# Linear attention followed by a two-layer network, one core: the store of x is queued right behind its multiplication, and the pools of on-chip memory begin at other addresses

## The chip, the cores and the metric

The kernel runs on one core of one Trainium2 chip. The metric is the device time of one execution in microseconds (us). The time before is the median of three runs, 1118.28 us (1115.12 to 1119.28).

## What is computed

Eight batches of eight heads, 576 positions, 64 values a head; then a network on the 4608 rows of 512 values that the attention gives.

```python
def phi(x):
    proj = np.einsum('bhsd,df->bhsf', x, w_phi)          # 64 -> 128 features
    proj = proj - np.max(np.abs(proj), axis=-1, keepdims=True)
    return np.concatenate([np.exp(proj), np.exp(-proj)], axis=-1)
q_p, k_p = phi(q), phi(k)
kv  = np.einsum('bhsf,bhsd->bhfd', k_p, v)
z   = np.sum(k_p, axis=2)
num = np.einsum('bhsf,bhfd->bhsd', q_p, kv)
den = np.einsum('bhsf,bhf->bhs', q_p, z)[..., None] + 1e-06
attn = num / den
# x: attn with the heads side by side, 4608 x 512
h = x @ w_in            # 512 -> 2048
g = h - np.tanh(h)
out = g @ w_out         # 2048 -> 512
```

## The kernel before

There are two stages. The first does the attention, unit by unit: a unit is two heads of one batch, and there are 32. The second does the network for nine groups of 512 rows, each in 16 steps over 128 of the 2048 hidden values.

**The first stage is a software pipeline written out by hand** (`manual_schedule`: each engine takes its instructions in the order of the code). `ramp` starts units 0 to 2, `period(i)` is called for i = 3 to 31, `drain` ends it. One call of `period` works on six units at once: `a` is unit i (projected), `c` is i-1, `p` is i-2 (its numerator is made), `r` is i-3 (its denominator is made and loaded), `q` is i-4 (its reciprocals are spread), `o` is i-5 (multiplied and stored).

The way of one unit through the steps that matter here:

- `num` (L327, PE) multiplies q's features with kv into the PSUM tile `po`. `num_copy` (L351, ACT) copies `po` into the tile `d`. `d` has three buffers (`bufs=3`), so the copy for unit p can only write once the buffer of unit p-3, which is `o`, has been stored.
- The bank of `po` is also the bank of `pa`: the last part of the next unit's `project` (L219, PE, `pa`) writes there, and so waits for `num_copy`.
- `denom` (L341, PE) and `ksum` (L299, PE) write the bank `pu`. `denom_copy` (L355, ACT) copies the denominators to `dd`, one buffer, out of the pool `tail`.
- `den_recip_load` (L360, a DMA on SP's queue) brings one row in 32 of `dd` into `dn`, nine numbers a partition; `den_recip` (L365, DVE) makes `rn`; `den_store` (L370, SP) writes it to `rr` in DRAM; a period later `den_spread` (L375, two DMAs on SP) reads `rr` back into `rb`, spread over 64 partitions a head.
- A period later again `den_mul` (L378, POOL) multiplies `d` by `rb` in place, and `x_store` (L381, SP) writes `d` to `xs` in DRAM, from where the second stage loads it. `rb` has one buffer, so the spread of unit q comes behind the multiplication of unit o.

SP's queue takes its DMAs in the order of the code: an instruction that waits holds those behind it. SP also loads `v` (L200). The loads of q and k (`qk`, L196) and of the weights (`rawi`, `rawo`) are issued by ACT.

**The second stage** keeps x and the weights as pairs of a high and a low part, three matmuls of 512 columns for each product (L606 for the first layer, L649, L650 and L652 for the second), with the polynomial and tanh on ACT and DVE and the split of g on ACT and POOL.

**Memory.** Pools are laid one behind the other along a partition: `consts`, `tail`, `wpool`, `wpa`, `xp0`, and behind them the pools of the first stage (`raw`, `p1`, `p2`), whose room the second stage's pools (`xp`, `wp`, `gp`, `gm`) take over. Tiles of `wpool`, `wpa`, `xp0`, `raw` and of the second stage are 2048 bytes a partition or multiples of it. In the kernel before `wpool` begins 1056 bytes past a multiple of 2048, and so do all these tiles. In `p1` the tiles `zt` (512 bytes) and `ones` (128 bytes) lie ahead of the two `kp` (10240 bytes each), which so begin 1696 bytes past one.

Of the kernel before, what the change touches and what calls it, by code (L numbers as in the profile page):

```python
# [8 lines left out]
F32 = mybir.dt.float32  # L9
# [10 lines left out]
P = 128  # L20
# [12 lines left out]
def tile_linear_attention_moe(  # L33
# [26 lines left out]
    CH = S // 2  # L60
# [3 lines left out]
    consts = ctx.enter_context(tc.tile_pool(name="consts", bufs=1))  # L64
# [1 line left out]

    ident = consts.tile([P, P], F32, name="ident")
    make_identity(nc, ident)
    bias_t = consts.tile([P, 4], F32, name="bias_t")
    nc.gpsimd.memset(bias_t[:, 0:1], PB1)  # L70
    nc.gpsimd.memset(bias_t[:, 1:2], PB2)
    nc.gpsimd.memset(bias_t[:, 2:3], -Y0)
# [1 line left out]
    tail = ctx.enter_context(tc.tile_pool(name="tail", bufs=2))  # L74
# [8 lines left out]
    def split_w(n, pin=lambda ins: ins):  # L83
        d, nm, f = (wi, wo)[n % 2], "io"[n % 2], n // 2
        early = f < AHEAD
        w = d[f]
        wh = (wpa if early else wp[0]).tile([P, DM], F32R, name=f"wh{nm}{f}")
        wl = wpool.tile([P, DM], F32R, tag="w", name=f"wl{nm}{f}")
        if early or nm == "i":
            pin(nc.scalar.copy(wh, w))  # L90
        else:
            pin(nc.vector.tensor_copy(wh, w))
        d[f] = (wh, wl)

        def low():
            pin(nc.gpsimd.tensor_tensor(wl, w, f32(wh), ALU.subtract))

        return low
# [25 lines left out]
    with ExitStack() as c1:  # L124
        raw = c1.enter_context(tc.tile_pool(name="raw", bufs=2))
        p1 = c1.enter_context(tc.tile_pool(name="p1", bufs=1))
# [65 lines left out]
        def load(u, queue=nc.sync):  # L192
            u.qk = p2.tile([P, PC], F32, tag="qk", name=f"qk{u.i}")
            cut = (0, PC) if u.i else (0, 4 * P, PC)
            for o, w in zip(cut, cut[1:]):
                queue.dma_start(u.qk[:, o:w], qkT[u.i][:, o:w])  # L196
# [6 lines left out]
        def project(u, parts):  # L203
            for part in parts:
                if part == "j":
                    u.t = [p2.tile([P, 2, 5, F], F32, tag="t0", name=f"t{u.i}_0"), None]
                    u.m = [p2.tile([P, 2, 5], F32, tag="m0", name=f"m{u.i}_0"), p2.tile([P, 2, 4], F32, tag="m1", name=f"m{u.i}_1")]
                    u.pj = ps_pj.tile([P, 2, 512], F32, tag="pj", name=f"pj{u.i}")
                    bank, tiles = u.pj, range(4)
                elif part == "t":  # L210
                    u.pt = ps_t.tile([P, 2, 512], F32, tag="pt", name=f"pt{u.i}")
                    bank, tiles = u.pt, range(4, 5)
                else:
                    u.pa = ps_d.tile([P, 2, 512], F32, tag="po", name=f"pa{u.i}")
                    bank, tiles = u.pa, range(5, 9)
                for k, a in enumerate(tiles):
                    for e in range(2):
                        hs = slice(e * D, (e + 1) * D)
                        nc.tensor.matmul(  # L219
                            bank[:, e, k * F : (k + 1) * F], u.qk[hs, a * P : (a + 1) * P], wph[hs, :], start=True, stop=True  # L220
                        )
# [10 lines left out]
        def centre(u, parts):  # L232
            for part in parts:
                x, m, t = part_of(u, part)
                nc.vector.tensor_reduce(m, x, AX.X, ALU.max, apply_absolute_value=True)  # L235
                nc.vector.tensor_tensor(t, x, m.unsqueeze(3).broadcast_to(list(t.shape)), ALU.subtract)  # L236
# [49 lines left out]
        def kadd(u):  # L286
            x = p2.tile([P, 2, 2, F], F32, tag="ss", name=f"ss{u.i}")
            nc.gpsimd.tensor_tensor(x, u.kp[:, :, 1], u.kp[:, :, 2], ALU.add)
            nc.gpsimd.tensor_tensor(x, x, u.kp[:, :, 3], ALU.add)
            nc.gpsimd.tensor_tensor(x, x, u.kp[:, :, 4], ALU.add)  # L290
            nc.gpsimd.tensor_tensor(x, x, u.kp[:, :, 0], ALU.add)
            u.ss = x
# [14 lines left out]
        def ksum_turn(u):  # L307
            nc.tensor.transpose(u.pu[:, 0:F], u.kst, ident)
# [42 lines left out]
            nc.scalar.copy(u.d.rearrange("p (c n) -> p c n", c=2), u.po[:, :, 0:CH])  # L351

        def denom_copy(u):
            u.dd = tail.tile([P, CH], F32, tag="dd", name=f"dd{u.i}", bufs=1)
            nc.scalar.activation(u.dd, u.pd, AF.Identity, bias=bias_t[:, 3:4])  # L355

        def den_recip_load(u):
# [19 lines left out]
        def den_mul(u, pin=lambda ins: ins):  # L377
            pin(nc.gpsimd.tensor_tensor(u.d, u.d, u.rb, ALU.mult))  # L378

        def x_store(u):  # L380
            nc.sync.dma_start(xs[u.b // 2][u.hp, :, (u.b % 2) * S : (u.b % 2 + 1) * S], u.d)  # L381

        units = []
        for i in range(B * NHP):
            u = Unit()
# [13 lines left out]
        def unit(i):  # L399
            return units[i] if 0 <= i < NU else None  # L400

        def bank():
            return ps_c.tile([P, 512], F32, tag="pu", name="pu")
# [48 lines left out]
        def period(i):  # L452
            a, c, p, r, q, o = (unit(i - n) for n in range(6))
            w = dec[i - 3]
            low = split_w(i - 4) if 4 <= i < 2 * AHEAD + 4 else None
            if o:
                den_mul(o)
            project(a, "jat" if i > 3 else "ajt")
            centre(a, "jt")
            kadd(c)  # L460
            if low:
                low()
            dec.append(dec_load(i - 2, nc.scalar))
            if i + 2 < NU:
                load(units[i + 2], nc.scalar)
            pu = bank()
            if r:
                denom(r, pu)
            ksum(p, pu)
            if r:  # L470
                denom_copy(r)
                den_recip_load(r)
            if q:
                den_spread(q)
            if o:
                x_store(o)
            if i > 3:
                load_v(a)
            ksum_copy(p)
            kv_turn(p)  # L480
            kv_turn_copy(p)
            dec_0(w, a.pt)
            q_turn(c)
            ksum_turn(p)
            q_turn_rest(c, pu)
            q_exp(c)
            q_exp_rest(c)
            ksum_turn_copy(p)
            centre(a, "a")
            k_exp(a, 0)  # L490
            kv(c)
            kv_copy(c)
            k_exp(a, 1, (0,))
            dec_1(w)
            dec_2(w)
            if r:
                den_recip(r)
                den_store(r)
            dec_3(w)
            if i == NU - 1:  # L500
                for j in range(NCT // 2):
                    x_split(xt[0], j)
            if i == NU - 2:
                xt[0] = x_tiles(0)
                for j in range(NCT):
                    x_load(0, xt[0], j)
            num(p)
            num_copy(p)
            if i < NU - 1:
                k_exp(a, 1, (1,))  # L510
# [9 lines left out]
        def drain():  # L520
            o, q, r, p, c = units[-5:]
            den_mul(o)
            pu = bank()
            denom(r, pu)
            ksum(p, pu)
            denom_copy(r)
            den_recip_load(r)
            den_spread(q)
            x_store(o)
            ksum_copy(p)  # L530
            k_exp(c, 1, (1,))
            kadd(c)
            den_mul(q)
            dec.append(dec_load(NU - 2, nc.scalar))
            kv_turn(p)
            kv_turn_copy(p)
            decode(dec[NU - 3], lambda: (den_recip(r), den_store(r)))
            q_turn(c)
            ksum_turn(p)
            q_turn_rest(c, pu)  # L540
            q_exp(c)
            ksum_turn_copy(p)
            q_exp_rest(c)
            kv(c)
            kv_copy(c)
            num(p)
            x_store(q)
            den_spread(r)
            den_mul(r)
            dec.append(dec_load(NU - 1, nc.scalar))  # L550
            for j in range(NCT // 2, NCT):
                x_split(xt[0], j)
            kv_turn(c)
            kv_turn_copy(c)
            pu = bank()
            ksum(c, pu)
            denom(p, pu)
            ksum_copy(c)
            num_copy(p)
            decode(dec[NU - 2])  # L560
            ksum_turn(c)
            ksum_turn_copy(c)
            denom_copy(p)
            den_recip_load(p)
            x_store(r)
            num(c)
            w = dec[NU - 1]
            dec_0(w, ps_t.tile([P, 2, 512], F32, tag="pt", name="pt"))
            num_copy(c)
            dec_1(w)  # L570
            dec_2(w)
            dec_3(w)
            denom(c, bank())
            denom_copy(c)
# [11 lines left out]
    with ExitStack() as c2:  # L586
# [86 lines left out]
        for i in range(len(steps) + 2):  # L673
            if i < len(steps):
                g, f = steps[i]
# [13 lines left out]
            if 1 <= i <= len(steps):  # L689
                g, f = steps[i - 1]  # L690
# [12 lines left out]
            if i >= 2:  # L703
                g, f = steps[i - 2]
# [61 lines left out]
```

## Time and profile before

| what | before |
|---|---|
| median of three runs | 1118.28 us (1115.12 to 1119.28) |
| profiled execution | 1114.96 us, of which its span is 1113.2 us and 1.8 us lie around it |
| granted TensorE clock | 0.998 |
| first stage | from 0 to 321.4 us of the span |
| second stage | from 321.4 us to the end |
| PE busy | 1096.1 us, 98% of the span |
| DVE busy | 837.9 us |
| ACT busy | 770.6 us |
| POOL busy | 441.0 us |

The span runs from the first to the last instruction of the profiled execution. PE is the matmul engine, PEld its weight load, DVE the vector engine, ACT the scalar engine, POOL the third compute engine and SP the engine that here issues DMAs only; SPq and ACTq are the instruction queues ahead of those engines. An entry such as "ACT d L351 <- DMA xs<-d" reads: ACT's instruction of line 351, which writes d, waited for the DMA that writes xs from d.

### The profile page before, as it was taken

The numbers are of one execution on the slowest core, as the hardware profiler recorded it, in microseconds if no ns is written. First come the engines' busy times: TensorE is split into PE (matmuls) and PEld (weight loads), VectorE is DVE, ScalarE is ACT, GpSimd is POOL, SyncE is SP. The second block draws the span as 40 slices with busy tenths as digits, with TensorE's granted clock in tenths as the row PEclk, the third lists the DMA queues.
The fourth block names the chain that finished last, engine by engine and source line by source line (L and its number), as shares of the span: only waits on it lengthen the run. The fifth ranks groups of instructions, "written<-read, shape, count | busy, mean of one in ns | idle before, by whom it ended". The sixth has DMA issues, their size and how long they took to land.

```text
span 1113.2 us, 18532 instructions
## 1 busy us (share of the span) xinstructions
PE 1096.1 (98%) x6956; PEld 864.5 (78%) x6956; DVE 837.9 (75%) x1166; ACT 770.6 (69%) x1394; POOL 441.0 (40%) x349
## 2 busy tenths in 40 slices
PE   8999999999999999999999999999999999999998
PEld 6676666676668888888888888888888888888886
DVE  6988889899988767767667767767767676676664
ACT  5787887777777766667666666666666666666664
POOL 4787877666645532322222222222222222222222
PEclk9999999999999999999999999999999999999999
DMA  5577777677740011011011010001002002000001
GB/s 184 168 207 208 214 209 216 207 220 221 204 144 1 1 54 34 22 49 39 1 38 38 1 38 38 1 10 66 1 1 76 1 1 76 1 1 38 1 1 39
DMA packets 51003, 85.46 MB, mean 77 GB/s; under 512 B 13280, under 2 KB 24672, under 8 KB 50912
## 3 DMA queue, kind: packets, MB, share of 16 engines
q1 hardware_dynamic: 36656, 52.02, 14.6%
q10 hardware_dynamic: 14256, 32.25, 9.9%
q8 instruction: 55, 0.90, 0.3%
q14 instruction: 36, 0.29, 0.1%
HBM read 65.08 MB, written 19.02 MB: 76 GB/s over the span
## 4 chain that ended last, share of the span: by engine, by line
PE 91%; DMA 2%; DVE 2%; ACT 2%; SPq 1%; POOL 1%; issue 1%; ACTq 0%; DVEq 0%; POOLq 0%
PE ph L606 34%; PE po L649 12%; PE po L652 12%; PE po L650 12%; PE pc L278 5%; PE po L327 4%; PE pu L341 3%; PE pa L219 3%; PE pj L219 3%; DMA xs<-d 2%; PE ptt L247 2%; PE pc L316 1%; DVE t L236 1%; DVE m L235 1%; PE pu L299 1%; ACT d L351 1%
## 5 line engine op out<-in xcount | busy, mean ns | idle before, releaser
L635 POOL TENSOR_TENSOR gl<-s,gh 128x512 fp32r<-128x512 f32 x144 | 186.1, 1293 | 556.0 <-ACT gh L634 547.5
L613 ACT ACTIVATE y<-ph 128x512 f32<-128x512 f32 x144 | 86.2, 598 | 254.2 <-PE ph L606 254.2
L622 DVE SCALAR_TENSOR_TENSOR s<-s,y 128x512 f32<-128x512 f32 x144 | 102.1, 709 | 186.5 <-ACT s L615 185.5
L649 PE MATMUL po<-who,gh 128*128 128x512 f32 x572 | 223.3, 390 | 1.8 <-ACT gh L634 1.8
L606 PE MATMUL ph<-xh,whi 128*128 128x512 f32 x576 | 224.3, 389 | 0.0
L606 PE MATMUL ph<-xh,wli 128*128 128x512 f32 x576 | 224.1, 389 | 0.0
L606 PE MATMUL ph<-xl,whi 128*128 128x512 f32 x576 | 224.1, 389 | 0.0
L650 PE MATMUL po<-wlo,gh 128*128 128x512 f32 x572 | 223.0, 390 | 0.0
L652 PE MATMUL po<-who,gl 128*128 128x512 f32 x572 | 153.7, 391 | 0.0
L628 DVE COPY_PREDICATED s<-mk,th 128x512 f32<-128x512 uint32 x128 | 122.8, 959 | 13.8 <-DVE th L627 0.9
L649 PEld LDWEIGHTS po<-who,gh 128*128 128x128 f32 x572 | 107.7, 188 | 25.1 <-ACT gh L634 2.7
L606 PEld LDWEIGHTS ph<-xh,whi 128*128 128x128 f32 x576 | 108.0, 188 | 23.3 <-DVE s L628 0.5
L606 PEld LDWEIGHTS ph<-xl,whi 128*128 128x128 f32 x576 | 108.2, 188 | 22.4
L652 PEld LDWEIGHTS po<-who,gl 128*128 128x128 f32 x572 | 108.0, 189 | 22.6
L606 PEld LDWEIGHTS ph<-xh,wli 128*128 128x128 f32 x576 | 108.1, 188 | 22.4
L650 PEld LDWEIGHTS po<-wlo,gh 128*128 128x128 f32 x572 | 107.6, 188 | 22.3
L615 ACT ACTIVATE s<-y,bias_t 128x512 f32<-128x512 f32 x144 | 104.4, 725 | 0.5 <-POOL gl L635 0.5
L621 ACT ACTIVATE mk<-y,bias_t 128x512 f32<-128x512 f32 x144 | 103.5, 719 | 1.4 <-DVE s L628 1.4
L625 DVE SCALAR_TENSOR_TENSOR s<-s,ph 128x512 f32<-128x512 f32 x144 | 98.9, 686 | 5.2
L624 DVE SCALAR_TENSOR_TENSOR s<-s,s 128x512 f32<-128x512 f32 x128 | 88.8, 694 | 15.9 <-ACT s L617 3.5
L272 ACT ACTIVATE kp<-t 128x1024 f32<-128x1024 f32 (+1 forms) x128 | 90.5, 731 | 8.9 <-DVE t L236 7.8
L617 ACT ACTIVATE s<-y,bias_t 128x512 f32<-128x512 f32 x128 | 92.4, 722 | 0.9 <-POOL gl L635 0.9
(98 smaller groups left out, 1693.7 us busy)
## 6 DMA issues: line engine op xcount, KB each, us to landing
qk<-in_qkT ACTq DMA_DIRECT2D x27, 576.0 KB
v<-in_v SPq DMA_DIRECT2D x32, 320.0 KB, 4.2
rb<-rr SPq DMA_DIRECT2D x64, 144.0 KB, 3.6
xs<-d SPq DMA_DIRECT2D x32, 288.0 KB, 3.5
out<-o SPq DMA_DIRECT2D x36, 256.0 KB, 2.3
rawo<-in_moe_w_out ACTq DMA_DIRECT2D x16, 512.0 KB, 3.9
rawi<-in_moe_w_in ACTq DMA_DIRECT2D x15, 512.0 KB, 4.1
xl<-xs SPq DMA_DIRECT2D x24, 256.0 KB, 3.2
```

The lines of the kernel that those rows point to most:

```text
L272: nc.scalar.activation(u.kp[h, :, j, s, :], u.t[r][h, :, x, :], AF.Exp, scale=1.0 - 2.0 * s)
L606: nc.tensor.matmul(h, wt[:, c * P : (c + 1) * P], x[:, c, 0:N], start=(i == 0), stop=(i == 3 * NCT - 1))
L615: nc.scalar.activation(s1, y, AF.Square, bias=bias_t[:, 0:1])
L617: nc.scalar.activation(s2, y, AF.Square, bias=bias_t[:, 1:2])
L621: nc.scalar.activation(mk, y, AF.Relu, bias=bias_t[:, 2:3])
L622: nc.vector.scalar_tensor_tensor(s1, s1, PC1, y, ALU.add, ALU.mult)
L625: nc.vector.scalar_tensor_tensor(gs, gs, PA, h, ALU.mult, ALU.mult)
L628: nc.vector.copy_predicated(gs, mk.bitcast(U32), hh)
L635: pin(nc.gpsimd.tensor_tensor(gl, gs, f32(gh), ALU.subtract))
L649: nc.tensor.matmul(po[t], a, wo[f][0], start=(f == 0), stop=False)
L650: nc.tensor.matmul(po[t], a, wo[f][1], start=False, stop=False)
L652: nc.tensor.matmul(po[t], gl[:, t * P : (t + 1) * P], wo[f][0], start=False, stop=(f == NF - 1))
```

## The change

Three edits.

1. `x_store(o)` is called right behind `den_mul(o)`, at the head of `period` and of `drain`. Before it stood behind `den_recip_load(r)` and `den_spread(q)`. Those two now stand behind it in SP's queue.
2. The tile `dd` (1152 bytes a partition) comes from `p1`, a pool of the first stage alone, and no longer from `tail`. It has one buffer as before.
3. `bias_t` is 28 columns wide and no longer 4 (96 bytes more a partition). The columns that are written and read are the same four. Together with edit 2 this takes 1152 - 96 = 1056 bytes out from ahead of `wpool`: it, `wpa`, `xp0`, `raw` and the second stage's tiles begin at multiples of 2048 bytes. The first `kp` begins 640 bytes past one.

```diff
-    bias_t = consts.tile([P, 4], F32, name="bias_t")
+    bias_t = consts.tile([P, 28], F32, name="bias_t")
...
         def denom_copy(u):
-            u.dd = tail.tile([P, CH], F32, tag="dd", name=f"dd{u.i}", bufs=1)
+            u.dd = p1.tile([P, CH], F32, tag="dd", name=f"dd{u.i}")
...
         def period(i):
             if o:
                 den_mul(o)
+                x_store(o)
...
                 den_recip_load(r)
             if q:
                 den_spread(q)
-            if o:
-                x_store(o)
             if i > 3:
                 load_v(a)
...
         def drain():
             den_mul(o)
+            x_store(o)
             pu = bank()
...
             den_recip_load(r)
             den_spread(q)
-            x_store(o)
```

SP's queue in one call of `period` (i = 7), the kernel before and after as one piece of the difference; `xs<-d` is the store of unit o, `dn<-dd` the load of unit r's denominators, `rb<-rr` the two DMAs that spread unit q's reciprocals, `v<-in_v` the load of unit a's v, and `rr<-rn` the store of unit r's reciprocals. The numbers behind the names are buffers.

```order
 L370 DMA rr_851<-rn_849 128x9
-L360 DMA dn_924<-dd_922 128x1x9
-L375 DMA rb_926<-rr_851 64x576 x2
 L381 DMA xs_76<-d_602 128x576
+L360 DMA dn_925<-dd_923 128x1x9
+L375 DMA rb_927<-rr_851 64x576 x2
 L200 DMA v_930<-in_v 128x640
```

The store has moved ahead of three DMAs, and they now stand behind its wait for POOL.

The same queue at the head of `drain`, where o is unit 27; the last row is the store of unit 28.

```order
-L360 DMA dn_4107<-dd_4105 128x1x9
-L375 DMA rb_4109<-rr_4072 64x576 x2
 L381 DMA xs_79<-d_3829 128x576
+L360 DMA dn_4108<-dd_4106 128x1x9
+L375 DMA rb_4110<-rr_4072 64x576 x2
 L370 DMA rr_4135<-rn_4133 128x9
 L381 DMA xs_79<-d_3960 128x576
```

Here too the store has passed the load and the two spreads. The order of instructions on PE, ACT, DVE and POOL is the same in both kernels.

## The prediction

> **What bounds the kernel now.** I read the head of the page first, for the span and the busy time of each engine, then the chain of work that ended last.
>
> ```profile
> span 1113.2 us, 18532 instructions
> PE 1096.1 (98%) x6956; PEld 864.5 (78%) x6956; DVE 837.9 (75%) x1166; ACT 770.6 (69%) x1394; POOL 441.0 (40%) x349
> PE 91%; DMA 2%; DVE 2%; ACT 2%; SPq 1%; POOL 1%; issue 1%; ACTq 0%; DVEq 0%; POOLq 0%
> ```
>
> PE carries 91% of the chain, so only time in which PE waits, or a faster PE, can move the end. The chain also passes through DMA, SP's queue and ACT (2 + 1 + 2%): somewhere a transfer holds PE up. The busy time by stage tells where. I cut the span at the end of two copies of L355, one in each turn of `period`, and at the first matmul of L606.
>
> ```profile
> core 0: us, PE busy (x) PEld busy (x) DVE busy (x) ACT busy (x) POOL busy (x), PEclk, DMA share, GB/s
> 0.00:40.47 40.47, 34.60 (x381) 24.85 (x382) 28.61 (x36) 24.23 (x45) 19.70 (x27) 1.00 0.51 161
> 40.47:301.45 260.98, 257.56 (x2946) 179.67 (x2945) 234.24 (x326) 205.52 (x393) 194.82 (x150) 1.00 0.71 210
> 301.45:321.40 19.95, 17.76 (x179) 10.49 (x176) 17.09 (x24) 14.77 (x32) 11.34 (x9) 1.00 0.64 211
> 321.40:1095.00 773.60, 773.50 (x3414) 639.82 (x3411) 551.91 (x775) 518.92 (x916) 211.28 (x162) 1.00 0.07 24
> ```
>
> In the second stage PE is busy for 773.50 of 773.60 us: nothing that only removes waits can help there. In the steady part of the first stage PE is also nearly full, but busy time takes in the modelled tails of matmuls, so I look at the waits of just that stretch (40 to 302 us).
>
> ```profile
> POOL d L378 <- DMA rb<-rr: 24.6, 18, 1.9
> PEld pa L219 <- ACT d L351: 5.0, 10, 1.0
> ACT d L351 <- DMA xs<-d: 4.0, 10, 0.7
> PE pa L219 <- ACT d L351: 2.7, 4, 0.8
> ACT d L351 <- PE pj L219: 2.4, 2, 1.3
> ```
>
> Here is the stall: PE's `pa`, and the weight load ahead of it, wait for `num_copy` (L351), and `num_copy` waits for a store of x that has not landed. One such turn in order of time, on SP, POOL and ACT, and then the chain through it:
>
> ```profile
> 199.86 1.42 POOL L378 TENSOR_TENSOR d<-d,rb 128x576 f32<-128x576 f32 x1 [1.79 <-DMA rb<-rr]
> 204.07 0.51 ACT L355 ACTIVATE dd<-pu,bias_t 128x288 f32<-128x288 f32 x1 [1.88 <-PE pu L299]
> 204.60 0.59 SPq L360 DMA_DIRECT2D dn<-dd  x1
> 205.37 1.19 SPq L375 DMA_DIRECT2D rb<-rr  x2
> 206.60 1.30 SPq L381 DMA_DIRECT2D xs<-d  x1
> 210.07 0.32 SPq L370 DMA_DIRECT2D rr<-rn  x1
> 211.24 0.64 ACT L351 COPY d<-po 128x576 f32<-128x576 f32 x1 [1.31 <-PE pj L219]
> ```
> ```profile
> 210.04 1.11 PE pj L219 x16
> ...
> 211.24 0.65 ACT d L351
> ...
> 211.93 1.16 PE pa L219 x16
> ```
> ```profile
> DMA to landing us min/median/max: 4.5/4.5/4.5
> ```
>
> The product was ready at 199.86 + 1.42 = 201.28. Its store was issued at 206.60: SP stood at the load of `dd`, which waited for ACT until 204.58, and then issued the spread. The store took 4.5 us to land (last row: that store alone), to 211.1, and `num_copy` began at 211.24. The wait's label, PE's `pj`, is the last semaphore event, but the landing fits the start to 0.1 us, so I count this row of 2.4 us with the 4.0.
>
> **The change part by part. The store moved (edit 1).** It can now be issued at about 201.3, 5.3 us earlier. Landing took 3.1 to 5.6 us in this stretch:
>
> ```profile
> L381 SPq DMA_DIRECT2D xs<-d x26: 583/585/1565, 51.9 to 293.8; - x26
> ...
> DMA to landing us min/median/max: 3.1/3.5/5.6
> ```
>
> Even with the longest it lands at 206.9, well before the copy of this turn can start. The copy needs the numerator, whose matmuls end with the start of `pj` at 210.04, so some 3 us are left. The wait goes. What is late next? Turns in which the store happened to be in time show it, four in a row, and one that waited:
>
> ```profile
> 157.34:166.69 9.35, 9.35 (x111) 6.58 (x109) 8.34 (x13) 7.90 (x16) 7.82 (x7) 1.00 0.78 228
> 166.69:176.11 9.42, 9.42 (x111) 6.56 (x110) 8.61 (x13) 7.28 (x15) 7.82 (x7) 1.00 0.73 215
> 176.11:185.53 9.42, 9.42 (x111) 6.55 (x110) 8.61 (x13) 7.28 (x16) 6.58 (x6) 1.00 0.71 215
> 185.53:194.96 9.43, 9.43 (x111) 6.58 (x110) 8.63 (x13) 7.30 (x16) 6.55 (x6) 1.00 0.69 215
> 204.58:215.21 10.63, 9.84 (x112) 6.64 (x110) 8.85 (x14) 7.39 (x15) 6.57 (x6) 1.00 0.69 199
> ```
>
> In the first four PE has no gap, DVE has 0.8 to 1.0 us to spare, and ACT and POOL more. So PE is next, at 9.35 us for the shortest turn and 37.62 / 4 = 9.405 for the four. The steady stretch holds 27 turns (one `num_copy` each):
>
> ```profile
> L351 ACT COPY d<-po x27: 620/638/640, 45.9 to 297.5; 128x576 f32<-128x576 f32 x27
> ```
>
> Its mean turn is 260.98 / 27 = 9.666 us. At 9.405 the gain is 27 x 0.261 = 7.0 us, at 9.35 it is 27 x 0.316 = 8.5 us. PE's own waits for the copy, 5.0 + 2.7 = 7.7 us, lie between. I take 7.5. The lower bound is 4.0 us, what the list of waits puts down to the store by name, if PE's other waits for the copy only change their cause.
>
> **What the store is moved past.** The load of `dd` and the two spreads now stand behind the store's wait for POOL. POOL ended at 201.28 and the load could not go before 204.58: 3.3 us of room, of which issuing the store takes SP 0.58 us in the median and 1.57 at most. At least 1.7 us are left, so load and spread go out when they did. The spread needed that product in any case, as `rb` has one buffer. On the DMA engines the store's 288 KB now come ahead of the load and the spread, not behind them. With a median landing of 3.5 us it has landed by 204.8, when the spread's first DMA is 0.6 us from issue: cost between 0 and the 1.5 us by which the longest landing (206.9 against 205.37) would run into it. I take 0, since POOL, which waits for the spread, has 1.5 us or more idle in each quoted turn. The load of `v` follows the spread directly, about 1.2 us sooner; no row has anybody waiting for it. I take 0.
>
> At the head of `drain` the room is smaller:
>
> ```profile
> 306.81 1.42 POOL L378 TENSOR_TENSOR d<-d,rb 128x576 f32<-128x576 f32 x1 [2.25 <-PE po L327]
> 308.28 0.50 ACT L355 ACTIVATE dd<-pu,bias_t 128x288 f32<-128x288 f32 x1
> 310.89 0.59 SPq L381 DMA_DIRECT2D xs<-d  x1
> ```
>
> The product ends at 308.23, the denominators' copy at 308.78. With 0.59 us for the issue the load goes out 0.05 us late, with 1.57 us 1.0 us late, once. PE does not read what it brings before the second stage, so I count 0 and keep 1.0 us for the range.
>
> **`dd` in another pool, `bias_t` wider (edits 2 and 3).** No instruction is added, and the copy to `dd` reads and writes as many bytes (0.51 us). What they change is addresses. The stage where that could matter is the second. There 3414 matmuls fill 773.60 us, 226.6 ns each, 0.443 ns a column of 512. In the first stage the numerator's matmuls did better per column:
>
> ```profile
> 160.65 1.94 PE po L327 x16
> ```
>
> 1.94 us / 16 / 288 columns is 0.421 ns. If the second stage's extra 0.022 ns a column came from where its tiles begin, 512 columns would take 215.6 ns, and 3414 x 11.0 ns = 37.6 us would go. What speaks against it: the numerator's `qe` lies at no multiple of 2048 either, and the slices of `kp` that L278 streams are 1024 bytes each, starting 1696 bytes past a multiple of 2048, so every second one crosses such a boundary.
>
> ```profile
> L278 PE MATMUL pc<-kp,v x286: 378/379/431, 159.8 to 294.8; 128*64 128x256 f32 x143
> ```
>
> From the least to the median is 1 ns: crossing costs nothing there. But those are other matmuls, and no tile of the second stage lies elsewhere, so the trace can't exclude it. I take 0 and keep 37.6 us as a rival; a loss of the same kind has no row at all.
>
> The Trainium skill (TensorE: Matmul & The Clock Gate, Back-to-back issue gap) has N/2.4 + 2.5 ns between warm matmuls, about 216 ns for 512 columns, and names no address in it; the measured 226.6 ns is above that, so by the Trainium skill there is something in this stage to win, an estimate of 3414 x 10.8 = 36.9 us. The Trainium skill (SBUF — State Buffer, Terms) has lines of 16 bytes in this memory; 1056 is a multiple of 16, so by the Trainium skill every tile began on a line already and the layout changes nothing. No run here shows either.
>
> **The sum.** 7.5 us out of the first stage, 0 for the rest. The profiled execution would go from 1114.96 to 1107.5 us. It lies 3.3 us below the median of the runs, just under the lowest of them. As the stall hangs on when a transfer lands, some of those 3.3 us may be the same stall; I count 0.8 of it, an estimate. 1118.28 - 7.5 - 0.8 gives 1110.0 us, 0.7% faster. About 0.5% (5.6 us) is what a measurement of this kernel tells from no change.
>
> **The rivals.** *Another wait takes the place.* If in turn after turn without the stall DVE or ACT fall behind, only the 4.0 us booked by name go: 1114.3 us, no change that can be told. For it speaks that DVE fills 8.3 to 8.6 of 9.4 us; against it the four turns in a row without a gap on PE. *The addresses speed up the second stage.* 37.6 us more: 1110.0 - 37.6 = 1072.4 us. For it speaks the rate per column, against it L278's row and `qe`. *SP is held by POOL: slower.* If products end later than the denominators' copy less the issue, the load goes out late. It is issued at 204.60, and the store of the reciprocals made of it at 210.07, 5.5 us later, so it has 1.4 us of slack if it lands in 4 us, more than the store's median for 288 KB. It decides when POOL's product comes 1.7 + 1.4 = 3.1 us later than now; DVE then stands in front of its reciprocal, and each us beyond costs up to 27 us. With one us a turn: 27 - 7.5 = 19.5 us more, 1137.8 us. POOL waited 1.9 us for the spread at worst, and that is inside the 3.3 us already, so it is unlikely. *The change does nothing*, the store being issued no earlier, would need a product that ends after 206: no quoted turn has it.
>
> **How the numbers follow.** Forecast (1106 to 1113 us) 0.69; another wait in its place 0.17; addresses speed up the second stage 0.09; SP held by POOL, or addresses that cost, 0.05. A few of the first case's hundredths (0.04) fall short of 0.5%. Faster: 0.69 + 0.09 - 0.04 = 0.74. Same: 0.17 + 0.04 = 0.21. Slower: 0.05. The range leaves out the two rivals far away (0.14) and a little at either end: low 1105, which is 1118.28 less 8.5 and less the 3.3 us between profile and median, with 1.5 us for scatter; high 1117, which takes in the case of another wait.
>
> **What would show it.** In the profile after, SP issues the store before the load of `dd`, about 0.1 us behind POOL's product. "ACT d <- DMA xs<-d" and "pa <- ACT d" are gone from the list of waits. The turns take 9.35 to 9.45 us throughout, the first matmul of L606 comes at about 314 us, and the second stage takes 773.6 us as before. I am wrong if the turns still exceed 9.5 us with another releaser, if matmuls of the second stage are spaced by other than 226.6 ns, or if the load of `dd` is issued more than 1 us behind its copy.

## The result, and the profile after

Six runs of the changed kernel take 1110.24 us in the median (1109.98 to 1110.71), six of the kernel before 1116.29 us (1114.06 to 1119.28). The ratio is 0.9941, 95% interval 0.993 to 0.9953: 0.6% faster. The runs after lie within 0.7 us, those before within 5.2 us. The profiled execution takes 1110.15 us, where that of before took 1114.96.

The head of the page after, and the chain of work that ended last:

```profile
span 1108.4 us, 18532 instructions
PE 1093.0 (99%) x6956; PEld 860.8 (78%) x6956; DVE 837.3 (76%) x1166; ACT 769.2 (69%) x1394; POOL 439.2 (40%) x349
PE 94%; DVE 4%; ACT 1%; DMA 1%; issue 0%; POOL 0%; POOLq 0%; ACTq 0%; DVEq 0%
```

The span is 4.8 us shorter. DMA and SP's queue have nearly left the chain. The busy time by stage, cut at the same events as before (columns as there):

```profile
0.00:40.78 40.78, 34.92 (x381) 25.24 (x382) 28.61 (x36) 24.23 (x45) 19.55 (x27) 1.00 0.50 160
40.78:296.29 255.51, 255.00 (x2945) 176.90 (x2944) 233.22 (x325) 203.73 (x392) 192.74 (x150) 1.00 0.71 214
296.29:316.38 20.09, 17.88 (x178) 10.44 (x176) 17.64 (x24) 14.82 (x32) 11.85 (x10) 1.00 0.66 215
316.38:1090.00 773.62, 773.55 (x3414) 639.82 (x3411) 551.75 (x775) 519.31 (x916) 211.18 (x162) 1.00 0.07 24
```

All of the gain lies in the 27 steady turns: 255.51 us against 260.98, 5.5 us less. The start is 0.3 us longer and the drain 0.1. The second stage takes 773.62 us for 3414 matmuls, 226.6 ns each, as before. The waits in the steady stretch (38 to 298 us):

```profile
POOL d L378 <- PE po L327: 26.1, 14, 2.9
POOL d L378 <- DMA rb<-rr: 19.2, 10, 3.0
PEld po L327 <- DVE t L236: 7.7, 27, 0.7
ACT d L351 <- issue: 0.5, 2, 0.3
DVE t L236 <- DVE m L235: 1.4, 3, 0.5
```

The copy no longer waits for the store, and `pa` no longer waits for the copy. One turn, the rows of POOL, SP and ACT that stood for before, with the loads that ACT issues:

```profile
198.32 1.41 POOL L378 TENSOR_TENSOR d<-d,rb 128x576 f32<-128x576 f32 x1 [2.66 <-DMA rb<-rr]
199.76 0.32 SPq L381 DMA_DIRECT2D xs<-d  x1
201.21 0.50 ACT L355 ACTIVATE dd<-pu,bias_t 128x288 f32<-128x288 f32 x1 [1.89 <-PE pu L299]
201.74 0.59 SPq L360 DMA_DIRECT2D dn<-dd  x1
...
198.26 0.33 ACTq L164 DMA_DIRECT2D rawo<-in_moe_w_out  x1
199.86 0.34 ACTq L196 DMA_DIRECT2D qk<-in_qkT  x1
```
```profile
L381 SPq DMA_DIRECT2D xs<-d x27: 319/319/577, 48.0 to 294.5; - x27
...
DMA to landing us min/median/max: 3.3/5.7/6.5
```

The store goes out 0.03 us behind its product (199.73), and the load of `dd` 0.03 us behind its copy (201.71). But the room between product and copy is 2.0 us here, not 3.3 (2.2 and 3.3 in the median over the 27 turns), and the store now takes 5.7 us to land in the median, not 3.5. The view of landings counts one load of x (5.6 us) with the 26 stores; the stores alone give the same three figures.

### The profile page after: what moved, and what is told of

The parts are those of the page before. It is cut to its first block, busy times and chain, and to the rows that moved or that the text cites. A ratio compares the mean times of both kernels' runs of the same rounds, so it can differ in the third digit from the quotient of the medians.

```text
span 1108.4 us, 18532 instructions
## 1 busy us (share of the span) xinstructions
PE 1093.0 (99%) x6956; PEld 860.8 (78%) x6956; DVE 837.3 (76%) x1166; ACT 769.2 (69%) x1394; POOL 439.2 (40%) x349
## 4 chain that ended last, share of the span: by engine, by line
PE 94%; DVE 4%; ACT 1%; DMA 1%; issue 0%; POOL 0%; POOLq 0%; ACTq 0%; DVEq 0%
PE ph L605 35%; PE po L648 11%; PE po L649 11%; PE po L651 11%; PE pc L278 6%; PE po L327 5%; PE pj L219 3%; PE pu L341 3%; PE ptt L247 2%; PE pa L219 2%; DVE m L235 1%; DVE t L236 1%; PE pc L316 1%; PE pu L299 1%; PE pt L219 1%; PE pu L252 1%
```

## The experiments

All times are medians; the kernel before took 1117.71 us (17 runs, 1113.16 to 1121.35) beside the first four and 1116.27 us (9 runs, 1113.36 to 1116.93) beside the others. The changed kernel was not run again beside them: its 1110.24 us are those of the section above.

**The store alone.** Edit 1 without edits 2 and 3:

```diff
             if o:
                 den_mul(o)
+                x_store(o)
...
-            if o:
-                x_store(o)
...
         def drain():
             den_mul(o)
+            x_store(o)
...
-            x_store(o)
```

> The store is issued behind its product as in the changed kernel; dd and bias_t are as in the kernel before, so the pools begin where they began before. Theory (the copy of the numerator waited for the store of the buffer it writes; the addresses do nothing): 1110.2 us within 0.6, turns of 9.42 us, runs within 1 us of each other. Rival (the addresses, by faster transfers, carry part of the gain): about 1113 us, and some waits of the copy for the store are left. Rival (the addresses cost, and hide a larger gain of the store): under 1109 us.

Measured: 1109.91 us (1109.67 to 1110.88), ratio to before 0.9931, interval 0.991 to 0.9952. Its steady stretch and its second stage:

```profile
40.90:296.50 255.60, 255.05 (x2945) 176.96 (x2944) 233.55 (x325) 203.55 (x393) 193.74 (x150) 1.00 0.72 214
316.63:1090.23 773.60, 773.51 (x3414) 639.78 (x3411) 551.91 (x775) 519.03 (x916) 211.33 (x162) 1.00 0.07 24
```

Both stages are those of the changed kernel to 0.1 us, though every tile begins where it began before. The store is the whole gain.

**The addresses alone.** Edits 2 and 3 without edit 1:

```diff
-    bias_t = consts.tile([P, 4], F32, name="bias_t")
+    bias_t = consts.tile([P, 28], F32, name="bias_t")
...
-            u.dd = tail.tile([P, CH], F32, tag="dd", name=f"dd{u.i}", bufs=1)
+            u.dd = p1.tile([P, CH], F32, tag="dd", name=f"dd{u.i}")
```

> dd in the first stage's pool and bias_t of 28 columns, the store where it was before. Theory: no change from before, 1116.3 us within 1.5, runs that scatter over some 4 us, and the copy's waits for the store are still there. Rival (addresses carry part): about 1113 us. In both the matmuls of the second stage stay 226.7 ns apart.

Measured: 1116.45 us (1113.82 to 1118.68), ratio 0.9985, interval 0.9971 to 0.9999: less than 0.3%, if anything. The stall is there, and the second stage is as long as ever:

```profile
ACT d L351 <- DMA xs<-d: 7.4, 12, 1.3
PEld pa L219 <- ACT d L351: 7.0, 11, 1.2
PE pa L219 <- ACT d L351: 4.7, 8, 1.0
```
```profile
39.94:303.04 263.10, 257.83 (x2946) 179.67 (x2945) 234.64 (x326) 205.33 (x393) 193.08 (x150) 1.00 0.70 208
323.00:1096.60 773.60, 773.52 (x3414) 640.04 (x3411) 551.70 (x775) 519.09 (x917) 211.29 (x162) 1.00 0.07 24
```

**A smaller dose: the store one place further on.** Addresses as before, in `period`:

```diff
+            if o:
+                x_store(o)
             if q:
                 den_spread(q)
-            if o:
-                x_store(o)
```

> Addresses as before; the store stands between the load of the denominators and the two spreads, in period alone. It is issued about 1.3 us sooner than before and some 4 us later than in the changed kernel. Theory: the waits of the copy were 1.3 us at most, so nearly all go: 1110.5 to 1112 us, turns of 9.42 to 9.5 us; the landing takes about 3.5 us as before. Rival (what helps is that the loads of v and the spreads follow one another, or that SP no longer holds the store behind the load's wait for ACT): no gain here, 1115 to 1118 us.

Measured: 1110.86 us (1109.79 to 1111.86), ratio 0.9936, interval 0.9913 to 0.996. Four short waits of the copy are left:

```profile
ACT d L351 <- DMA xs<-d: 1.7, 4, 0.6
```

The landing was forecast at 3.5 us. Only one store in this stretch has a landing time in the profile, 3.9 us, so I went by the trace's single packets (a store is 128 packets of 2304 bytes). In the median of units 3 to 25 the store was issued 0.7 us behind the copy to `dd`, against 1.95 before, and its last packet ended 2.6 us behind the issue, against 1.9. So of the 1.2 us won at the issue some 0.5 us were left at the end.

Passing the two spreads alone brings nearly all of the gain. What counts is that the data arrive a little sooner, not the queue's order as such.

**A dose the other way: the store one place later.**

```diff
             if i > 3:
                 load_v(a)
+            if o:
+                x_store(o)
```

(and not ahead of `load_v`).

> Addresses as before; in period the store stands behind the load of v, one place later than before. It is issued about 0.7 us later and its 288 KB come behind 320 KB of v in the queue, about 1.5 us at the 210 GB/s of this stretch. Theory: before, the store landed about when it was needed, so nearly each of the 27 turns grows by the 1 to 2.2 us that it lands later: 1140 to 1175 us. Rival (the copy's wait is hidden behind other work and the gain came from elsewhere): within 5 us of before.

Measured: 1175.06 us (1174.16 to 1177.79), ratio 1.0516, interval 1.0488 to 1.0544; the upper end of what was forecast. Waits (40 to 298 us, about 22 turns) and the steady stretch:

```profile
ACT d L351 <- DMA xs<-d: 38.0, 20, 3.3
PEld pa L219 <- ACT d L351: 37.0, 21, 3.2
PE pa L219 <- ACT d L351: 33.0, 21, 3.0
```
```profile
40.97:359.04 318.07, 274.48 (x2946) 189.47 (x2945) 238.44 (x326) 205.96 (x393) 195.56 (x151) 0.95 0.60 175
```

A turn takes 318.07 / 27 = 11.78 us, 2.1 us more than before. The copy waits for its buffer in most turns, and PE for the copy. The granted clock is 0.95 in this stretch, at which a turn of 9.42 us would take 0.5 us more (an estimate), so a part of the 2.1 us may be slower matmuls.

**The wait taken away without moving the store.** The kernel before, with a fourth buffer for `d`:

```diff
-            u.d = tail.tile([P, S], F32, tag="d", name=f"d{u.i}", bufs=3)
+            if u.i % 4 == 3 and u.i < 24:
+                x = xp0.tile([P, NCT, G * P], F32R, tag="xl", name=f"d{u.i}")
+                u.d = f32(x).rearrange("p c n -> p (c n)")[:, 0:S]
+            else:
+                u.d = tail.tile([P, S], F32, tag="d", name=f"d{u.i}", bufs=3)
```

> The kernel before, addresses and order of SP's queue as they were; every fourth unit up to unit 23 takes its d from a tile of x that is free in the first stage, so a buffer of d is written again four units later and not three. Theory (the copy waited for its buffer): a turn more leaves 9 us of room, the waits of the copy for the store go without the store being moved, turns of 9.42 us up to about the 24th unit, and the last ones as before: 1110.2 to 1112 us. Rival (the gain needs the store ahead of the load and the spread in the queue): no gain, 1115 to 1119 us.

Measured: 1110.53 us (1109.70 to 1110.85), ratio 0.9953, interval 0.994 to 0.9965. The steady stretch is 255.91 us:

```profile
40.83:296.74 255.91, 255.30 (x2946) 177.18 (x2945) 233.35 (x325) 203.75 (x392) 194.59 (x150) 1.00 0.71 214
```

The store goes out and lands as late in the turn as it did before: 5.1 us behind its product in the median, against 5.25, and 3.5 us later it has landed, as before.

This settles the mechanism. With the store and SP's queue untouched the same time goes, and so does the scatter (1.2 us over five runs).

**Why the store now lands late.** The changed kernel without every second load of q and k:

```diff
-            if i + 2 < NU:
+            if i + 2 < NU and i % 2 == 0:
                 load(units[i + 2], nc.scalar)
+            elif i + 2 < NU:
+                units[i + 2].qk = units[i + 1].qk
```

> The changed kernel with the load of q and k left out in every second period (two units then share what was loaded, so their results are those of other inputs). For the landing of the store, 5.7 us in the changed kernel against 3.5 before. Theory (the 576 KB of q and k and the 512 KB of weights that ACT issues just ahead share the DMA engines with it): the store lands after about 3.5 to 4 us in the turns without that load and still 5 to 6 us in the others. Rival (the place in SP's queue makes it slow): 5 us and more in all turns. The time stays within 1 us of 1110.2 in both, since nothing waits for the landing.

Measured: 1109.45 us, one run. Its profile has no landing times for the store, so I took them from the trace's single packets: the store's are the first 128 of 2304 bytes behind its issue. (The last packet ends ahead of the landing: 4.6 us behind the issue in the changed kernel's median, where the landing takes 5.7, and 1.9 us in the kernel before, where it takes 3.5.) For the stores of units 3 to 25 the last of them ended within 3.3 us in 10 of 23 turns, the least being 2.0; in the changed kernel in 1 of 23, the others taking 3.4 to 5.7 us. Up to unit 13 short and long strictly alternate (2.6, 5.1, 2.6, 5.9, 3.3, 5.0, 2.3, 5.2, 3.0 from unit 4 on), and the short ones are the turns without the load.

Behind unit 13 the forecast fails as it stands: units 14, 20, 22 and 24 take 3.7 to 4.8 us without that load, and units 19, 21 and 23 take 2.0 us with it. What tells them apart is what ACT's queue had been given before the store. I counted the data of that queue whose packets started between the store's issue and its last packet:

| turns | ACT's data in between | last packet behind the issue |
|---|---|---|
| without the load of q and k, units 4 to 12, 16, 18 | 428 to 504 KB | 2.3 to 3.3 us |
| without it, units 14, 20, 22, 24, 25 | 512 KB | 3.7 to 4.8 us |
| with it, issued within 0.2 us of the store, units 3 to 13, 15, 17 | 576 to 1052 KB | 4.3 to 5.9 us |
| with it, but issued about 0.5 us behind the store, units 19, 21, 23 | 19 to 24 KB | 2.0 us |
| kernel before, units 3 to 25 | 4 to 121 KB | 1.6 to 2.2 us |

In the units of the second row the weights were issued 0.3 to 1.3 us ahead of the store, in those of the first 1.3 to 2.1 us, so more of them had been moved by then. So it is the loads that ACT issues just ahead of the store or together with it (`rawo` 512 KB and `qk` 576 KB by the page, at 198.26 and 199.86 in the turn shown, the store at 199.76), and not the place in SP's queue, that make it slow: from the same place it takes 2.0 us when they come behind it.

**How near the slow rival was.** The changed kernel with the load of the denominators behind the spread and the load of v:

```diff
                 denom_copy(r)
-                den_recip_load(r)
             if q:
                 den_spread(q)
             if i > 3:
                 load_v(a)
+            if r:
+                den_recip_load(r)
```

> The changed kernel with the load of the denominators behind the spread and the load of v in SP's queue: issued about 2 us later and behind 320 KB of v. It measures how near the slow rival was. By the prediction's 1.4 us of room the reciprocal on DVE waits 0.6 us or more a turn and up to 3 us with the queueing; DVE has some 0.8 us to spare in a turn, so turns grow by 0 to 2.4 us: 1110 to 1175 us, and if the load lands as late as the store now does, 1140 us or more. Rival (room far above 2 us): within 1 us of 1110.2.

Measured: 1122.16 us (1118.40 to 1122.46), ratio to before 1.0059, interval 1.0044 to 1.0074, so about 12 us behind the changed kernel. The profiled execution is the fastest of the four, 1118.40 us:

```profile
DVE rn L365 <- DMA dn<-dd: 20.5, 21, 2.1
```
```profile
40.00:304.47 264.47, 259.01 (x2945) 177.59 (x2944) 232.31 (x325) 204.22 (x393) 192.56 (x150) 1.00 0.69 207
```

DVE stands in front of its reciprocal for 1 us in 21 of the 27 turns. Of these 20.5 us the steady stretch shows 9.0 (264.47 against 255.51); the rest fell into time that DVE had to spare. The load was not issued 2 us later, as was expected: it left SP 0.4 us behind its copy in the median, 2.05 at most. But it came behind the spread and `v` on the DMA engines, and its last packet ended 5.5 us behind that copy, where it was 3.1 us in the changed kernel. A delay of 2.3 us for a wait of 20.5 / 27 = 0.8 us a turn leaves a room of about 1.5 us, an estimate. It is not there in every turn: in the store-alone kernel, as fast as the changed one, DVE waits for this load five times,

```profile
DVE rn L365 <- DMA dn<-dd: 1.8, 5, 0.5
```

by half a microsecond at most, inside DVE's spare time.

**What is late next.** The changed kernel with the copy of the turned kv made by ACT:

```diff
-            nc.vector.tensor_copy(u.kv.rearrange("p a c -> p (a c)"), u.pc[:, 2 * P : 4 * P])
+            nc.scalar.copy(u.kv.rearrange("p a c -> p (a c)"), u.pc[:, 2 * P : 4 * P])
```

> The changed kernel with the copy of the turned kv (0.41 us on DVE) made by ACT. For the 9.42 us of the turns where PE alone needs 9.35, and the three turns of 9.8. Theory (PE's numerator waits for DVE's last step on pa, which shares its bank, and that copy stands ahead of it): turns of 9.35 us throughout, 27 x 0.07 + 3 x 0.4 = 3 us less, about 1107 us. Rival (PE's own 9.42 us, as when the weight load of one matmul is late): 1110 us.

Measured: 1108.55 us (1107.88 to 1109.04), ratio to before 0.9936, interval 0.9923 to 0.9948: faster than the kernel before, and 1.7 us under the changed one's 1110.24, which was not run beside it. The profiled spans are 1106.7 us against 1108.4, and 1.2 us of that lies in the steady stretch:

```profile
40.80:295.14 254.34, 254.34 (x2945) 179.34 (x2944) 224.63 (x298) 208.41 (x420) 192.98 (x150) 1.00 0.72 215
```

PE has no gap left in it, and yet a turn takes 254.34 / 27 = 9.42 us, not 9.35. Half of the forecast held: the three long turns are gone, and the numerator's weight load no longer waits for DVE (7.7 us over 27 turns in the changed kernel), but the 9.42 stayed. One turn of 9.66 us is new, and has another cause: in it `pa` waits for ACT, which has the 27 copies more to make.

```profile
PEld pa L219 <- ACT d L351: 0.2, 1, 0.2
```

As far as the profile shows, 9.42 us is PE's own.

## Why the prediction was right, and where its sizes were off

**The stall and its cause** were as forecast. `num_copy` waited for the store of the buffer three units back, `pa` waited for `num_copy`, and the chain is undone by moving the store or by a fourth buffer, and deepened by delaying the store.

**What the store gives, 7.5 us: too much.** The profiled execution gained 4.8 us, the steady stretch 5.5, and the first matmul of L606 came at 316.4 us, not at 314. Two steps were off. The first is the turn that would be left. I took 9.405 us from four turns in a row, with 9.35 as the floor. The turns after:

```profile
164.03:173.45 9.42, 9.42 (x111) 6.55 (x110) 8.62 (x13) 7.29 (x15) 7.66 (x7) 1.00 0.79 217
173.45:182.87 9.42, 9.42 (x111) 6.54 (x110) 8.61 (x13) 7.28 (x16) 6.97 (x6) 1.00 0.68 203
182.87:192.29 9.42, 9.42 (x111) 6.54 (x110) 8.61 (x13) 7.29 (x16) 6.14 (x6) 1.00 0.68 232
201.71:211.49 9.78, 9.63 (x111) 6.55 (x110) 8.62 (x13) 7.40 (x16) 6.83 (x6) 1.00 0.64 192
```

24 of the 27 take 9.42 to 9.43 us, and no turn 9.35. The turns of 9.35 before each came behind a longer one, as the first of my four did (9.63): they paid back, and were no floor. At 9.42 the gain would have been 27 x (9.666 - 9.42) = 6.6 us. The other 1.1 us are three turns of 9.8, of which my sample of four had none. The list of waits before had them too, hidden among larger ones.

The second is the 7.7 us that led me from 7.0 to 7.5. It adds PEld's wait and PE's, but these are the weight load and the matmul of the same `pa` in front of the same copy, so the sum counts one stall twice. In the turn shown they waited 1.0 and 0.8 us, and that turn was 10.63 - 9.42 = 1.2 us too long, not 1.8. PEld's 5.0 us alone would have been near the 5.5 that came.

**From the profile to the median: too little.** I counted 0.8 of the 3.3 us between the profiled execution and the median of three. With the store moved, or with the added buffer, the runs scatter by 0.7 to 1.2 us; one place on by 2.1 us, and in the old place by 3.6 to 8.2 us. That points to the same stall, larger in other runs: the addresses-alone kernel, whose profiled execution took 1.4 us more than that of before, has 263.10 us in its steady stretch against 260.98, and 7.4 us of the copy's waits for the store against 4.0. But a part of the 3.3 us was the chance of which three runs: six runs of before have their median at 1116.29 us, 1.3 above the profiled one. The gain taken too large (by 2.7 us) and this distance taken too small (by 2.4) nearly cancel in 1110.0 us against 1110.24, and that closeness is luck. Against the six-run median the change is worth some 6 us, not 8.3.

**What the store was moved past: 0, and it was 0,** but the room was used. In the turn shown the product comes about 1.2 us later in the turn than before: it starts 5.3 us behind the issue of its spread (193.01), where it was 4.1 (195.76), and POOL absorbs that in its idle time. The load of `dd` had some 1.5 us of room, about the 1.4 that I gave it, though its last packet now ends 3.1 us behind the copy and no longer 2.4. At the head of `drain` the product ended at 304.35 and the copy at 303.81, so the load went out 0.98 us behind its copy. I had kept 1.0 us for that in the range, for another reason (a long issue); the drain is 0.1 us longer.

The forecast of the landing from the median of another place in the turn was the weak step: 5.7 us came out. The 5.6 that I took as the longest was misread besides. It belongs to a load of x, which the view counts with the stores; the stores of before took 4.5 us at most:

```profile
DMA to landing us min/median/max: 2.1/3.5/4.5
```

Neither did harm, with the copy at 207.5 for a store issued at 199.76.

**The addresses: 0.** The rival by which they speed up the second stage is excluded by the windows of all four combinations: 773.60 to 773.62 us. The rate per column that spoke for it was no fair comparison. The numerator's 16 matmuls (form 128*64, the second stage's are 128*128) start in pairs 7 ns apart, a pair every 243 ns, so 0.421 ns is the mean over two that run side by side, and one of them takes 0.84 ns a column. What the Trainium skill (TensorE: Matmul & The Clock Gate, Back-to-back issue gap) gives for 512 columns as the gap of an isolated warm matmul, 216 ns, is not reached in this stage at either layout: 226.6 ns. That it adds nothing to begin on a coarser boundary agrees with the 16-byte lines of the Trainium skill (SBUF — State Buffer, Specifications (TRN2)), though no run here shows such a line.

**Rivals.** That another wait takes the place did not happen beyond the three long turns. That SP is held by POOL did not happen; the late load shows that it was about 1.5 us away.

## What to carry to other kernels

When a copy waits for a buffer whose store is stuck in a queue behind someone else's wait, issue the store as soon as its product exists, or give the tile one more buffer: either took the whole stall here, and the scatter between runs with it. For what a stage will cost once a stall is gone, take turns that follow an undisturbed turn; one that follows a late turn runs short. A transfer moved to another place in a turn meets other transfers there, so its time to land must be estimated from what is issued just ahead of it and beside it, and not from where it stood.

## What was not expected

The same store took 3.5 us to land where it stood and 5.7 us five microseconds earlier in the turn, beside up to 1.1 MB of loads issued by another queue. SP spent 0.32 us to issue it there (median, 319 ns), against 0.58 us behind the two spreads.

The three long turns are 8 turns, some 76 us, apart, in the kernel before as in the changed one. In each, DVE's `t<-pa` begins 0.46 to 0.51 us behind the reduction that it needs, where other turns have no such gap:

```profile
202.27 1.22 DVE L235 TENSOR_REDUCE m<-pa 128x8 f32<-128x1024 f32 x1
203.95 1.23 DVE L236 TENSOR_TENSOR t<-pa,m 128x1024 f32<-128x1024 f32 x1 [0.46 <-DVE m L235]
```

Between one of these gaps and the next lie 128 of DVE's recorded instructions, semaphore instructions counted. That speaks for something that goes by the count of instructions. But with kv's copy on ACT, which takes one instruction out of each of DVE's turns, no such gap is left in the steady stretch, and the cause stays open.
